# A load of down-projection weights issued as three transfers by partition range, in a decode block of attention and gated MLP

## The chip, the cores and the metric

The kernel runs on one core of one Trainium2 chip. The metric is the device time of one execution in microseconds; before the change it is 1279.16, the median of 3 runs (1279.07 to 1279.24). The engines are named as in the profile: PE does matmuls (PEld is its weight load), DVE and ACT are the vector and scalar engines, POOL is GpSimd, and SP only issues DMAs and waits. Data moves between HBM and SBUF (128 partitions) over 16 DMA engines.

## The reference

One token for each of 4 batch rows goes through attention over a cache of 8192 keys, with 32 heads of 128, and then through a gated MLP of width 1792. Both parts add to their input.

```python
def _A_ref(x, k_cache, v_cache, wq, wo):
    B, Sq, D = x.shape                      # 4, 1, 512
    H, Dh = 32, 128
    q = (x @ wq).reshape(B, Sq, H, Dh).transpose(0, 2, 1, 3)
    scores = jnp.einsum("bhqd,bhkd->bhqk", q, k_cache) * (Dh ** -0.5)
    p = _softmax(scores, axis=-1)
    o = jnp.einsum("bhqk,bhkd->bhqd", p, v_cache)
    return o.transpose(0, 2, 1, 3).reshape(B, Sq, H * Dh) @ wo

def _B_ref(x, w_gate, w_up, w_down):
    g = jnp.einsum("bsd,df->bsf", x, w_gate)
    u = jnp.einsum("bsd,df->bsf", x, w_up)
    return jnp.einsum("bsf,fd->bsd", _sigmoid(g) * u, w_down)

h = x + _A_ref(_layernorm(x), ...)
h2 = h + _B_ref(_layernorm(h), ...)
```

All inputs are bf16. The two caches are 268 MB each and make up nearly all of the bytes.

## The kernel before

The 128 pairs of batch row and head are worked off in 32 units of 4 heads. For each unit the keys (8 MB) and the values (8 MB) are loaded by one DMA each (L538) into one of three slots of the buffer KV; each partition gets 64 KB in one run. DVE transposes the keys in 16 steps (L334), PE makes the scores (L343), ACT the exponentials (L368), and PE multiplies with the values (L404) one unit later. All loads are issued by SP, in the order of one list, each as soon as its slot is free; a load waits in the DMA queue behind the bytes that were issued before it.

At the end the slots are used again for weights. When the last unit's keys have been read, SP issues the output projection (L543), the gate weights (L545) and the up weights (L549) into slot 1. When the values of the unit before the last have been read, it issues the down weights into slot 2 (L554). In SBUF the down weights are 14 tiles of 128 partitions by 512 columns, `wd_v`; partition p holds rows 14p to 14p + 13 of the matrix, 1 KB each. The tuple `WDT = (0, 8, 12, 14)` cuts them into three loads: tiles 0 to 7, 8 to 11 and 12 to 13, or 8 KB, 4 KB and 2 KB for each partition. Each has a semaphore of its own, `t_wd[i]`, and a DMA that has landed adds 16 to its semaphore. The last values are in slot 0 and are read after that.

After the attention the rest is a chain of small steps: output projection (L474), sum and layer norm (L479 to L286), gate (L493) with its sigmoid on ACT (L504), up projection, product and transposes in two halves on DVE (L510, L513), and the down projection on PE, line L518: 28 matmuls, two for each of the 14 tiles, one for each half of the 512 output columns, placed side by side in the array. A tile's matmuls wait for the half of the transposed product that they need and for the load that brings the tile:

```python
for t in range(NFT):
    if t == 0:
        filler(4)
    t_d = emit("pe", down(t), [t_hh[2 * t // NFT], t_wd[[t < v for v in WDT[1:]].index(True)]], incs=2)
```

So tiles 0 to 7 wait for the first load, 8 to 11 for the second, 12 and 13 for the third. DVE then adds the residual (L526), and two small DMAs, one issued by SP and one by ACT (L556), write the output. `prog.token(key, by)` makes a pair of a semaphore and the value to wait for, `by` above the last one; `prog.dma(engine, key, fn, waits, tok)` puts a DMA on an engine's list with a completion that adds 16, and returns the token.

## Time and profile before

| | before |
|---|---|
| median of 3 runs | 1279.16 us (1279.07 to 1279.24) |
| the profiled execution, its own time | 1279.28 us |
| span from the first to the last instruction in it | 1278.0 us |
| granted TensorE clock, mean | 0.814 |
| down weights: issue to landing of the three loads | 32.0, 32.9, 33.1 us |

The page of the profile gives busy time of each engine as a sum and by 40 slices of the span, then the DMA queues, the chain of waits that ended last, groups of instructions by line, and the DMA issues with the time from issue to landing. A busy share is a mean over stages; the chain and the windows of the last stage tell what sets the end.

### The profile page before, as it was taken

How to read it: one execution, taken by the hardware profiler on the slowest of the kernel's cores; microseconds unless marked ns; L12 is line 12 of the kernel's file. 1: busy time of each engine (PE TensorE's matmuls, PEld its weight loads, DVE VectorE, ACT ScalarE, POOL GpSimd, SP SyncE). 2: the span in 40 equal slices, each digit the busy share in tenths (PEclk: the TensorE clock that was granted, in tenths of full speed). 3: DMA queues.
4: the chain of work that ended last, by engine and by line, in shares of the span. 5: the costliest groups of instructions: out<-in, count | busy, mean ns of one | idle time of the engine just before them, and what ended most of it. 6: DMA issues, size and time to landing. Idle time of an engine off the chain costs nothing.

```text
span 1278.0 us, 14081 instructions
## 1 busy us (share of the span) xinstructions
PE 782.9 (61%) x4590; PEld 328.4 (26%) x4641; DVE 762.3 (60%) x917; ACT 58.7 (5%) x114; POOL 5.7 (0%) x22
## 2 busy tenths in 40 slices
PE   1676765557755557655567655567555576555577
PEld 0232222223222223222222222222222232222233
DVE  1876665556665557665567655566655566655571
ACT  2000000000000000000000000000000000000001
POOL 1000000000000000000000000000000000000000
PEclk8788877788877788777788777888777888777889
DMA  9999999999999999999999999999999999999998
GB/s 425 429 425 429 427 449 435 427 429 429 453 429 427 429 435 447 429 429 427 445 437 429 429 427 449 433 429 429 427 449 435 427 429 431 449 431 427 429 437 360
DMA packets 10252, 550.83 MB, mean 431 GB/s; under 512 B 1148, under 2 KB 1160, under 8 KB 1416
## 3 DMA queue, kind: packets, MB, share of 16 engines
q1 hardware_dynamic: 10232, 550.77, 99.7%
q8 instruction: 2, 0.03, 0.0%
q14 instruction: 2, 0.02, 0.0%
q10 hardware_dynamic: 16, 0.01, 0.0%
HBM read 550.77 MB, written 0.00 MB: 431 GB/s over the span
## 4 chain that ended last, share of the span: by engine, by line
DMA 60%; PE 20%; DVE 12%; issue 2%; ACT 1%; SPq 0%; DVEq 0%
DMA KV<-in_A_k_cache_dram 58%; PE PS L343 15%; DVE kT L334 12%; PE PS L404 5%; DMA KV<-in_B_w_down_dram 3%; ACT kT L409 1%; PE PS L414 0%; SPq L538 0%; DVE PTz L374 0%; PE PS L518 0%; DVE KV L526 0%; SPq L554 0%; DVEq L112 0%
## 5 line engine op out<-in xcount | busy, mean ns | idle before, releaser
L343 PE MATMUL PS<-kT,Lq 128*128 128x512 bf16 x2048 | 592.0, 422 | 342.6 <-DVE kT L334 325.5
L334 DVE STREAM_TRANSPOSE kT<-KV 128x1024 f32<-128x1024 f32 x512 | 614.2, 1231 | 302.7 <-DMA KV<-in_A_k_cache_dram 237.9
L343 PEld LDWEIGHTS PS<-kT,Lq 128*128 x2048 | 211.0, 103 | 696.4 <-issue 624.2
L374 DVE STREAM_TRANSPOSE PTz<-E_sb 32x512 bf16<-32x512 bf16 x128 | 89.9, 703 | 128.9 <-PE PS L414 125.2
L404 PE MATMUL PS<-KV,PTz 128*16 128x512 bf16 x2048 | 116.9, 381 | 0.0
L378 PE MATMUL PS<-part,headw 128*128 128x2 f32 x64 | 18.8, 363 | 100.5 <-DVE PTz L374 100.5
L368 ACT ACTIVATE E_sb<-PS,negm 128x512 bf16<-128x512 f32 x32 | 22.0, 687 | 1141.7 <-DVE negm L366 1141.7
L404 PEld LDWEIGHTS PS<-KV,PTz 128*16 128x16 bf16 x2048 | 57.7, 109 | 57.3 <-issue 13.6
L414 PE MATMUL PS<-lane,kT 128*128 128x4 f32 x256 | 33.6, 255 | 31.0 <-ACT kT L409 31.0
L361 DVE TENSOR_REDUCE part<-PS 128x1 f32<-128x512 f32 x32 | 22.1, 691 | 38.8 <-PE PS L343 38.8
L414 PEld LDWEIGHTS PS<-lane,kT 128*128 128x128 f32 x256 | 31.0, 191 | 46.3 <-issue 44.9
L378 PEld LDWEIGHTS PS<-part,headw 128*128 128x128 f32 x64 | 16.0, 311 | 103.7 <-DVE PTz L374 103.7
L409 ACT ACTIVATE kT<-PS,rsb 128x512 f32<-128x512 f32 x32 | 22.0, 687 | 64.3 <-PE PS L404 64.3
L387 PE MATMUL PS<-Lq 128*128 128x512 bf16 x33 | 12.1, 425 | 2.7 <-issue 2.0
L453 DVE TENSOR_TENSOR kT<-PS,mask 128x512 bf16<-128x512 f32 x1 | 0.7, 690 | 16.1 <-PE PS L414 16.1
L327 DVE TENSOR_TENSOR Lq<-q_all,mask 128x32 bf16<-128x32 bf16 x32 | 9.7, 302 | 0.0
L387 PEld LDWEIGHTS PS<-Lq 128*128 128x128 bf16 x53 | 5.5, 109 | 8.9 <-issue 5.1
L366 DVE STREAM_TRANSPOSE negm<-mxr 128x32 f32<-128x32 f32 x32 | 6.8, 212 | 1.1
L363 DVE STREAM_TRANSPOSE turn<-part 128x32 f32<-128x32 f32 x32 | 6.8, 212 | 1.1
L395 DVE RECIPROCAL rsb<-PS 128x1 f32<-128x1 f32 x32 | 6.5, 202 | 0.7 <-PE PS L378 0.7
L321 PEld LDWEIGHTS PS<-Lq,headw 128*128 128x128 bf16 x32 | 3.4, 106 | 12.7 <-issue 11.2
L364 DVE TENSOR_SCALAR_CACHE_REDUCE turn<-turn 128x32 f32<-128x32 f32 x32 | 6.0, 186 | 1.1
(67 smaller groups left out, 52.6 us busy)
## 6 DMA issues: line engine op xcount, KB each, us to landing
KV<-in_A_wq_dram SPq DMA_DIRECT2D x1, 4096.0 KB, 12.4
KV<-in_A_wo_dram SPq DMA_DIRECT2D x1, 4096.0 KB, 26.9
KV<-in_B_w_gate_dram SPq DMA_DIRECT2D x1, 1792.0 KB, 31.0
KV<-in_B_w_up_dram SPq DMA_DIRECT2D x1, 1792.0 KB, 34.8
KV<-in_B_w_down_dram SPq DMA_DIRECT2D x1, 1024.0 KB, 32.0
KV<-in_A_k_cache_dram SPq DMA_DIRECT2D x32, 49.7
KV<-in_A_v_cache_dram SPq DMA_DIRECT2D x32, 30.8
KV<-in_B_w_down_dram SPq DMA_DIRECT2D x1, 512.0 KB, 32.9
```

Of the source, the lines that this page charges most:

```text
L327: t_lq[u] = emit("dve", lambda e, ix: e.tensor_tensor(dst, bass.AP(raw(q_all), at(ix, 0) * (4 * TU) + 4 * (u - TU * t), [[NU * 4, 128], [1 ...
L334: t_tr[u, c] = emit("dve", lambda e: e.transpose(kT[:, (c % 2) * TW:(c % 2 + 1) * TW], KVw[:, o:o + TW]), w, ch="d2p")
L343: ins = e.matmul(bank[SBK], bass.AP(raw(Lq), ix[-1] * 2 + (128 * t + c % 2), [[528, 128], [1, 128]]), rhs, start=False, stop=False, skip_g ...
L361: a = emit("dve", lambda e: e.tensor_reduce(part[:, 0:1], bank[SBK], AX.X, ALU.max), [t_sc[u, NT - 1], t_pool], ch="d2d")
L363: a = emit("dve", lambda e: e.transpose(turn_[:, :], part[:, :]), [a], ch="d2d")
L368: t_exp[u] = emit("act", lambda e: e.activation(E_sb[:, :], bank[SBK], ACT.Exp, bias=negm[:, 0:1], scale=SCALE, accum_out=part[:, 1:2]), [ ...
L374: return [e.transpose(PTz[32 * q:32 * (q + 1), :].rearrange("p (r q c) -> p r q c", r=4, q=4)[:, :, q, :], E_sb[32 * q:32 * (q + 1), :].re ...
L378: t_sum[u] = emit("pe", lambda e: e.matmul(bank[QB[1]][:, 0:2], headw[:, :], part[:, 0:2], start=True, stop=True), [t_ptz[u], t_selc], ch= ...
L387: emit("pe", lambda e: [e.matmul(bank[XS], Lq[:, 0:128], Lq[:, 0:512], start=True, stop=True) for _ in range(n)][-1], [t_ps0, t_lq[NU - 1] ...
L404: made.append(e.matmul(PS[32 * j:32 * j + 16, ob:ob + 512], lhsT, KV[:, slot * SLOT + 512 * k:slot * SLOT + 512 * (k + 1)], start=(k < 4), ...
L409: t_ocp[u] = emit("act", lambda e: e.activation(O_sb, bank[OBK], ACT.Copy, scale=rsb[:, 0:1]), [t_pv[u], t_rs[u]], ch="a2p")
L414: ins = e.matmul(bass.AP(raw(PS), at(ix, 0) * 4 + (512 * EX + 4 * (u - t)), [[4096, 128], [1, 4]]), O_sb[:, 128 * q:128 * (q + 1)], lane[: ...
```

## The change

The second load of the down weights, tiles 8 to 11, is issued as three DMAs in a row, of partitions 0 to 63, 64 to 115 and 116 to 127. All three add to the semaphore of the second load, whose token is now for 16 x 3 = 48. The first and the third load are one DMA each as before. The bytes, their places in SBUF, the waits ahead of the issues and the order of the instructions on the other engines are the same; SP has two instructions more.

```diff
-        t_wd = [prog.token(f"wd{i}", 16) for i in range(len(WDT) - 1)]
+        WDP = [(0, 128), (0, 64, 116, 128), (0, 128)]
+        t_wd = [prog.token(f"wd{i}", 16 * (len(WDP[i]) - 1)) for i in range(len(WDT) - 1)]
...
         for i in range(len(WDT) - 1):
-            prog.dma("sp", f"wd{i}", lambda e, i=i: e.dma_start(
-                wd_v[:, WDT[i]:WDT[i + 1], :], wd_src[:, WDT[i]:WDT[i + 1], :]), [v_done], tok=t_wd[i])
+            for a, b in zip(WDP[i], WDP[i][1:]):
+                prog.dma("sp", f"wd{i}", lambda e, i=i, a=a, b=b: e.dma_start(
+                    wd_v[a:b, WDT[i]:WDT[i + 1], :], wd_src[a:b, WDT[i]:WDT[i + 1], :]), [v_done], tok=t_wd[i])
```

## The prediction

> **What bounds the kernel now.** I read four views in this order: the profile's page for the whole span, the chain of waits over the last 37 us, the DMA issues, and short windows of the end for what the DMA engines still do there. The page first: the busy shares, the row by slices, the queues and the total.

> ```profile
> span 1278.0 us, 14081 instructions
> PE 782.9 (61%) x4590; PEld 328.4 (26%) x4641; DVE 762.3 (60%) x917; ACT 58.7 (5%) x114; POOL 5.7 (0%) x22
> DMA  9999999999999999999999999999999999999998
> q1 hardware_dynamic: 10232, 550.77, 99.7%
> q10 hardware_dynamic: 16, 0.01, 0.0%
> HBM read 550.77 MB, written 0.00 MB: 431 GB/s over the span
> ```

> The DMA engines are at 9 tenths or more in 39 of 40 slices and in the fortieth at 8; no compute engine is above 61%. The kernel is as long as its bytes, and then as the few us between the last byte and the last instruction. The change leaves every byte as it is, so only those few us are open. The chain of waits shows them (start us, length us, what):

> ```profile
> 1240.44 0.70 ACT kT L409
> ...
> 1241.70 0.33 SPq L554
> 1242.02 0.04 issue
> 1242.07 32.92 DMA KV<-in_B_w_down_dram
> 1274.98 0.04 issue
> 1275.03 0.60 PE PS L518 x8
> 1275.63 0.04 issue
> 1275.67 0.43 PE PS L518 x4
> 1276.10 0.02 issue
> 1276.12 0.42 DVE KV L526
> ```

> The second load of the down weights is itself a link: issued at 1242.07, it lands at 1242.07 + 32.92 = 1274.99, and 8 matmuls that wait for it (tiles 8 to 11) start at 1275.03. The last 4 (tiles 12 and 13) start at 1275.67. The DMA issues tell whether they waited for their own load (out<-in, queue, count, KB, us to landing), and the instructions in order of time give the issues' own places:

> ```profile
> KV<-in_B_w_down_dram SPq DMA_DIRECT2D x1, 1024.0 KB, 32.0
> KV<-in_B_w_down_dram SPq DMA_DIRECT2D x1, 512.0 KB, 32.9
> KV<-in_B_w_down_dram SPq DMA_DIRECT2D x1, 256.0 KB, 33.1
> ```

> ```profile
> 1241.70 1.28 SPq L554 DMA_DIRECT2D KV<-in_B_w_down_dram  x3
> 1273.87 2.18 PE L518 MATMUL PS<-KV 128*4 128x256 bf16 x28 [0.68 <-DMA KV<-in_B_w_down_dram]
> 1275.03 0.31 PEld L518 LDWEIGHTS PS<-KV 128*4 128x4 bf16 x8 [0.41 <-DMA KV<-in_B_w_down_dram]
> 1275.67 0.09 PEld L518 LDWEIGHTS PS<-KV 128*4 128x4 bf16 x4 [0.33 <-DMA KV<-in_B_w_down_dram]
> 1276.56 0.35 SPq L556 DMA_DIRECT2D out_dram<-KV  x1
> ```

> The first load lands at 1241.70 + 32.0 = 1273.7 and the third, issued some 0.85 us into the 1.28 us of the three issues, at 1242.55 + 33.1 = 1275.65: both later groups of matmuls wait for DMA, for 0.41 and 0.33 us by the idle time of the weight loads. What sets the end is therefore the last DMA engine to finish the second load and then the third. How many engines is that? Windows of the tail give the mean share of the 16 engines in use (the number ahead of GB/s; the DMA share times 16 is the number of engines):

> ```profile
> 1273.40:1273.80 0.40, 0.00 (x0) 0.00 (x0) 0.36 (x2) 0.00 (x0) 0.00 (x0) 1.00 0.74 282
> 1273.80:1274.20 0.40, 0.33 (x7) 0.30 (x9) 0.17 (x1) 0.00 (x0) 0.00 (x0) 1.00 0.32 123
> 1274.20:1274.50 0.30, 0.30 (x10) 0.26 (x6) 0.00 (x0) 0.00 (x0) 0.00 (x0) 1.00 0.16 61
> 1274.50:1274.90 0.40, 0.40 (x8) 0.10 (x3) 0.00 (x0) 0.00 (x0) 0.00 (x0) 1.00 0.13 51
> 1275.10:1275.30 0.20, 0.20 (x6) 0.16 (x8) 0.00 (x0) 0.00 (x0) 0.00 (x0) 1.00 0.03 10
> ```

> 0.74 is 12 engines, 0.32 is 5, 0.16 is 2.6 and 0.13 is 2.1. So some twelve engines are through with everything near 1274.0, and two run on alone to about 1275.2. The end waits for two late engines; the others have about 1.1 us to spare. This is the picture on which everything below rests.

> **The change, part by part.** Two more issues on SP. One of the three issues costs 1.28 / 3 = 0.43 us, so two add 0.86 us to SP, which then ends its issues near 1243.8. The transfers land 30 us later behind queued bytes, and SP's next instruction, the output's issue, is at 1276.56: cost nothing. The cover is the load's wait in the queue of 32 us; without it the third load would start 0.86 us late. Nothing is queued behind a new wait: SP gets none, and PE waits at the same place for one semaphore, at 48 in place of 16.

> The rows per engine. Transfers of 128 partitions are even: the page's 10232 packets on queue 1 are 71 loads of 128 rows and 16 completions (71 x 144 = 10224) and 8 packets of the output. The load of x, 4 partitions, used 4 engines:

> ```profile
> DMA packets 24, 0.53 MB, mean 264 GB/s; under 512 B 4, under 2 KB 8, under 8 KB 8
> q10 hardware_dynamic: 8, 0.00, 0.7%
> ```

> These are the first 3 us: 8 packets on the queue of that load, 4 rows and 4 completions. I take it that a load is dealt in equal shares to as many engines, up to 16, as divide its rows: 64 rows go as 4 to each of 16, 52 as 4 to each of 13, 12 as 1 to each of 12. [...] Against 8 rows each before, twelve engines get 9, one gets 8, three get 4. A row of the second load is 4 tiles of 512 bf16, 4096 B; an engine moves 431 / 16 = 26.9 GB/s, so a row takes 0.152 us. Twelve engines are 0.15 us longer, three are 4 x 0.152 = 0.61 us shorter.

> Which engines are the two late ones? No view numbers them. By count alone both are among the three relieved with 3/16 x 2/15 = 1/40, and at least one is among the twelve lengthened in 1 - 4/16 x 3/15 = 19 of 20. So the value that I take is: a late engine gets one row more. Landing of the second and of the third load +0.15 us, both groups of matmuls with it, and what follows (0.43 + 0.02 + 0.42, then the output) as it is. The 25 completions more, at most two an engine, have no price in any row; not counted.

> The pace of a piece that covers part of the partitions is not in the trace. Below: no loss, an engine's 26.9 GB/s holds, the sum above. Above: a piece goes at the full 431 GB/s times its share of the 128 partitions; then each of the three takes as long as the whole did, 524288 B / 431 GB/s = 1.22 us, 3.65 us in place of 1.22, that is +2.4 us for an engine in the middle of it. I take a value near the lower end, +0.2 instead of +0.15, since the late engines pass when the body has left. Body engines start the load together and could hinder one another, but have 1.1 us to spare; a late engine comes 1.1 us behind them.

> [...]

> Sum: +0.2 us on the profiled execution's own 1279.28 (its span of 1278.0 and 1.28 around it). That execution stands 0.12 above the median of the runs, 1279.16; on the median the forecast is 1279.35.

> **The rivals.** First, *both late engines are the relieved ones*. They finish the second load 0.61 us sooner. But PE then sets the pace: 8 matmuls, four pairs side by side, take 0.60 us with 0.27 of it the last one's duration (272 ns):

> ```profile
> L518 PE MATMUL PS<-KV 128*4 128x256 bf16 x28 | 2.0, 272 | 0.8 <-DMA KV<-in_B_w_down_dram 0.7
> ```

> a pair each (0.60 - 0.27) / 3 = 0.11 us. Fourteen pairs from 1273.87 without a wait end at 1273.87 + 13 x 0.11 + 0.27 = 1275.57; now they end at 1276.10. So at most 0.5 us is to be had: 1278.65. For it: two engines alone make the tail. Against it: three engines of sixteen must be the right ones.

> Second, on the other side, *the pieces run at a part of the rate*: the body engines crowd into the same part of SBUF, first the 16 together, then 13, then 12. Price: up to +2.4 us on the body, which is done near 1274.0 to 1274.1, so 1276.4 to 1276.5 in place of 1275.2: +1.3 us, 1280.45. It decides from 1.1 us of hindrance; with the 1.7 us that lies halfway between 1.1 and the upper end the time is +0.6, 1279.8. If the late engines are hindered as much as the body, the whole +2.4 us counts: 1281.55. For it: the loads now use all partitions at once and run at 431 GB/s, so nothing shows a spare rate. Against it: the engines are spread over 1.1 us, and pieces of different parts overlap.

> Third, *the pieces go to few engines*: 52 rows on 4 engines are 13 each; with 4 and 3 of the other pieces 20 in place of 8, 12 x 0.152 = 1.8 us; the body comes to 1275.9, +0.7, and if a late engine is one of them +1.8: 1279.85 to 1280.95. On one engine, 52 + 12 + 4 = 68 rows, 60 x 0.152 = 9.1 us: about +8, 1287. Against it: the load of x, split evenly.

> Fourth, *nothing to be seen*: the late engines keep their 8 rows, or the 0.15 falls in the scatter of 1279.07 to 1279.24: 1279.16.

> **How the numbers follow.** A late engine gets a row more, with little hindrance (the forecast, 1279.35): 0.45, and nothing to be seen 0.10. Both relieved: 0.12. Part of the rate: 0.25, of which 0.04 at the far end. Few engines: 0.08, of which 0.03 at one engine. The range goes from the first rival's 1278.65 to 1280.3, where the second's middle and the mild end of the third lie within; above it are about 0.10, below it a few hundredths. A difference under 0.2% (2.56 us) is about what a measurement of this kernel can tell from no change. No case is faster by as much, since PE alone stops the gain at 0.5 us: 0.02 for what I don't see. Slower by as much are one engine, and the far end of the second with something added: 0.03 + 0.04 = 0.07. Within it the rest, 0.91.

> **What would show it.** The packets of queue 1 tell the dealing: 64 + 16 + 52 + 13 + 12 + 12 = 169 in place of 144, so 10257 in all; 10240 would be 4 engines. The window of 1274.5 to 1274.9 tells the late engines: about 2 engines as now, with the tail some 0.15 us longer, if they got a row more; under 1 if both were relieved; 6 or more if the body was held up. The chain should still end through the second and third of the loads and PE, with 8 matmuls at about 1275.2. The forecast is wrong if the weight loads of tiles 8 to 11 no longer wait for DMA, or if the share between 1273.4 and 1274.2 is far above 0.74 and 0.32.

## The result and the profile after

The changed kernel takes 1281.39 us, median of 21 runs (1280.88 to 1282.2); the kernel before, run beside it, 1279.31 (1279.07 to 1279.94). The ratio is 1.0016, 95% interval 1.0011 to 1.0022: slower by 2.1 us, and no run of the one falls among the runs of the other. The forecast was +0.2 us with a range to 1280.3. The profiled execution of the changed kernel took 1281.94 us, 0.55 above its median.

The page of the changed kernel, in two of the rows shown of before:

```profile
span 1280.7 us, 14083 instructions
q1 hardware_dynamic: 10257, 550.77, 99.6%
```

Two instructions more, the same bytes, 25 packets more. The chain of waits at its end (start us, length us, what):

```profile
1241.70 33.84 DMA KV<-in_B_w_down_dram
1275.54 0.14 issue
1275.68 3.19 PE PS L519 x28
1278.87 0.02 issue
1278.89 0.42 DVE KV L527
```

Two things are new. The load at the head of the chain is now the first one (issued at 1241.70), which the change does not touch. It lands at 1275.54; before, it landed at 1273.73. And all 28 matmuls now stand in one piece of 3.19 us, which was 8 in 0.60 and 4 in 0.43 at the end of a group that began at 1273.87. The windows of the end show what the DMA engines do meanwhile (us, then busy time and count of PE, PEld, DVE, ACT, POOL, the granted clock, the DMA share, GB/s):

```profile
1272.00:1273.00 1.00, 0.84 (x7) 0.31 (x4) 0.62 (x2) 0.01 (x1) 0.00 (x0) 1.00 1.17 180
1273.40:1273.80 0.40, 0.00 (x0) 0.00 (x0) 0.36 (x2) 0.00 (x0) 0.00 (x0) 1.00 0.78 200
1273.80:1274.20 0.40, 0.00 (x0) 0.00 (x0) 0.10 (x1) 0.00 (x0) 0.00 (x0) 1.00 1.05 220
1274.50:1274.90 0.40, 0.00 (x0) 0.00 (x0) 0.00 (x0) 0.00 (x0) 0.00 (x0) 1.00 0.87 143
```

In 1272 to 1273 the kernel before moved 424 GB/s:

```profile
1272.00:1273.00 1.00, 0.84 (x11) 0.31 (x4) 0.55 (x2) 0.13 (x1) 0.00 (x0) 1.00 1.05 424
```

Now the DMA engines are as busy (share 1.17) and move 180. From 1274.5 to 1274.9, where two engines were left, 0.87 x 16 = 14 are at work. So the engines do not wait; each packet takes longer, as the counts below show. Both signs that the prediction named for being wrong are there: the share between 1273.4 and 1274.2 is 0.78 and 1.05 for 0.74 and 0.32, and the matmuls of tiles 8 to 11 no longer stand apart. Windows of a full us from the same view tell of PE:

```profile
1274.00:1275.00 1.00, 0.00 (x0) 0.00 (x0) 0.00 (x0) 0.00 (x0) 0.00 (x0) 1.00 0.85 156
1275.00:1276.00 1.00, 0.32 (x4) 0.25 (x6) 0.00 (x0) 0.00 (x0) 0.00 (x0) 0.64 0.46 131
1276.00:1277.00 1.00, 1.00 (x14) 0.62 (x10) 0.00 (x0) 0.00 (x0) 0.00 (x0) 0.50 0.16 61
```

PE had nothing to do from 1273.1 to 1275.68. The clock that it was granted fell to 0.50 during this wait, near 1275.3 (0.64 is the mean of the window from 1275 to 1276), and was still there when its matmuls ran. The group shows the price, and the length of the wait:

```profile
L519 PE MATMUL PS<-KV 128*4 128x256 bf16 x28 | 3.1, 414 | 2.6 <-DMA KV<-in_B_w_down_dram 2.6
```

A matmul takes 414 ns where it took 272.

Where the packets' time went can be counted in the trace by size: 8192 B rows (one packet each) belong to the first load, 4096 B to the second, 2048 B to the third. Nanoseconds of one packet, median / 90th percentile / longest, and the us at which the sixteen engines completed the first load:

```
                8192 B          4096 B          2048 B
before          313/319/321     159/169/172      84/ 89/ 94
after           314/332/853     294/426/486     144/200/248

first load, completions 1 to 12, and the last four
before          1272.07 to 1272.55     1272.85  1272.94  1273.57  1273.73
after           1271.84 to 1272.62     1274.01  1274.17  1275.25  1275.54
```

Twelve engines finish the first load as before. The four late ones are still in it while the twelve are in the pieces. Nine rows of the first load began after 1272.0, and all nine ended after 1272.62, so they belong to the late engines: they took 493 to 853 ns, where the last nine before took 309 to 321. The last row ended at 1274.71 for 1273.31, and its completion came 0.83 us behind it for 0.42: together that is the hold-up of 1.8 us.

### The profile page after: what moved, and what is told of

Its sections match the earlier page's. It is cut to its first block, busy times and chain, and to the rows that moved or that the text cites. A ratio compares the mean times of both kernels' runs of the same rounds, so it can differ in the third digit from the quotient of the medians.

```text
span 1280.7 us, 14083 instructions
## 1 busy us (share of the span) xinstructions
PE 780.8 (61%) x4590; PEld 328.7 (26%) x4641; DVE 763.2 (60%) x917; ACT 58.7 (5%) x114; POOL 5.7 (0%) x22
## 3 DMA queue, kind: packets, MB, share of 16 engines
q1 hardware_dynamic: 10257, 550.77, 99.6%
HBM read 550.77 MB, written 0.00 MB: 430 GB/s over the span
## 6 DMA issues: line engine op xcount, KB each, us to landing
KV<-in_A_wo_dram SPq DMA_DIRECT2D x1, 4096.0 KB, 26.9
KV<-in_B_w_down_dram SPq DMA_DIRECT2D x1, 1024.0 KB, 33.8
KV<-in_B_w_down_dram SPq DMA_DIRECT2D x2, 256.0 KB, 34.0
```

## The experiments

Each was run beside the kernel before; the time of that is 1279.23 in all. The 95% intervals of the ratios are about 0.001 to each side (1.2 us), so for differences under that the verdict rests on landings and packets of the profiled execution and on whether the ranges of the runs overlap. The kernel before took 1278.98 to 1280.46 in all of these; the runs with partitions 0 to 63, the third load, the 12 rows and 32 to 95 first overlap that range.

**Three transfers over all partitions.** The number of issues and the shared semaphore of the change, without its cut by partitions.

```diff
-WDP = [(0, 128), (0, 64, 116, 128), (0, 128)]
+WDP = [(0, 8), (8, 10, 11, 12), (12, 14)]
...
-wd_v[a:b, WDT[i]:WDT[i + 1], :], wd_src[a:b, WDT[i]:WDT[i + 1], :]
+wd_v[:, a:b, :], wd_src[:, a:b, :]
```

> The second load as three transfers on one semaphore again, but each over all 128 partitions (tiles 8 and 9, tile 10, tile 11). Theory (a piece that covers part of the partitions crowds the engines, which also slows the late engines that still work on the first load): here nothing is crowded, the first load lands near 1273.8 us as before the change, the time is that of before within 0.3 us. Rival (three issues and three completions on one semaphore cost by themselves): about +2 us, as in the changed kernel.

Measured: 1279.21 (1279.12 to 1279.42), ratio 0.9999 (0.999 to 1.0009). The first load landed at 1273.68 and the chain ends as before:

```profile
1242.35 32.62 DMA KV<-in_B_w_down_dram
1274.98 0.04 issue
1275.02 0.60 PE PS L519 x8
```

So two more issues and a wait for 48 cost nothing that shows; the cut by partitions costs it all.

**Halves.** No engine gets more rows than another: from 1235 us on there are 136 packets under 512 B for 120 before, the 16 completions of one more load on 16 engines.

```diff
-WDP = [(0, 128), (0, 64, 116, 128), (0, 128)]
+WDP = [(0, 128), (0, 64, 128), (0, 128)]
```

> Two pieces, partitions 0 to 63 and 64 to 127; every engine has 4 + 4 rows as before, none is lengthened or relieved. Theory (crowding): the first load still lands 1.5 us or more late, at 1275.2 or after, and PE starts its down matmuls after 2.3 us or more of idle; +1.2 to +2.2 us. Rival (the loss comes from the twelve engines with a ninth row): no difference, within 0.3 us.

Measured: 1281.41 (1280.79 to 1282.26), ratio 1.0015 (1.0005 to 1.0025), and the first load landed at 1276.39. All of the loss is there with 4 + 4 rows on every engine: the ninth row of twelve engines, and the relief of three, on which the forecast was built, can't be seen beside it.

**Partitions 0 to 63 alone, and 32 to 95 alone.** Same bytes, same rows for each engine, one transfer each; what differs is the place in SBUF, and with it which rows of the matrix are read. Both leave out half of the second load.

```diff
-WDP = [(0, 128), (0, 64, 116, 128), (0, 128)]
+WDP = [(0, 128), (0, 64), (0, 128)]         # the first
+WDP = [(0, 128), (32, 96), (0, 128)]        # the second
```

> Only partitions 0 to 63 of the second load are moved, by one transfer of 64 rows; partitions 64 to 127 of tiles 8 to 11 are left out. Half the bytes, so 0.6 us less for each engine if nothing crowds. Theory (crowding): single rows of 4096 B take up to about 0.4 us in place of 0.16, and the first load lands 0.8 us or more later than before. Rival (64 rows as such are no slower): the first load lands near 1273.75, the second and third 0.6 us sooner, and the time is 0.3 to 0.5 us under before.

> As the kernel with partitions 0 to 63 alone, but the 64 rows are partitions 32 to 95; the others of tiles 8 to 11 are left out. [...] Rival (any piece of 64 rows crowds, by its number of partitions): the same as with partitions 0 to 63, the first load 0.8 us or more late.

Measured: 1279.99 (1279.5 to 1280.23) and 1278.79 (1278.53 to 1278.95); the ranges lie 0.55 us apart. With 0 to 63 the 4096 B rows took 241 ns in the median and 461 at most, and the first load landed at 1274.65; with 32 to 95 they took 159 and 169, and it landed at 1273.76. In the chains of both kernels, the first and then the second, no load but the first is left:

```profile
1241.42 33.23 DMA KV<-in_B_w_down_dram
1274.65 0.14 issue
1274.78 1.74 PE PS L519 x28
```

```profile
1241.88 31.88 DMA KV<-in_B_w_down_dram
1273.76 0.14 issue
1273.89 1.74 PE PS L519 x28
```

So of two pieces of 64 partitions one was slow, with 241 ns a row, and one was not, with 159 ns: it is not the number of partitions in a piece that counts, but which they are. Whether SBUF or the reading from HBM makes the difference, no run separates; the halves of the up weights below, which are another matrix, were slow as well (172 to 229 GB/s).

**The changed kernel with PE kept busy.** 16 instead of 4 filling matmuls stand ahead of the down projection.

```diff
         if t == 0:
-            filler(4)
+            filler(16)
```

> The changed kernel with 16 instead of 4 idle-time matmuls ahead of the down projection (about 3.4 us of them, to near 1275.6), so that PE is not idle while it waits for the first load. Theory: in the changed kernel PE's granted clock fell to 0.50 because it had been idle for 2.6 us, and the 28 matmuls at that clock, 3.2 us, set the end. With the filling the clock stays at 1.00, the matmuls wait for the third load near 1277.6 and end 0.43 us after it: 0.6 to 0.9 us under the changed kernel, 1280.5 to 1280.8. Rival (the end is set by the landings alone, the clock is a side effect): no difference from the changed kernel, 1281.4.

Measured: 1281.06 (1280.78 to 1281.6), ratio 1.0013 (1.0004 to 1.0022). The clock stayed at 1.00, and the end went back to waiting for the loads:

```profile
1243.15 34.26 DMA KV<-in_B_w_down_dram
1277.41 0.04 issue
1277.46 0.60 PE PS L519 x8
```

The mechanism was as expected; the median is 0.33 us under the changed kernel's, about half of what was expected, and the ranges overlap. It was run again with the changed kernel next to it on one chip:

> The changed kernel once more, beside its copy with 16 filling matmuls, on one chip. Theory (idle PE costs it the full clock): +2.0 to +2.3 us over before, and 0.3 us or more above the copy with the filling. Rival (the clock is a side effect): the same time as the copy, within 0.15 us.

> The copy with 16 filling matmuls ahead of the down projection, on the same chip. Theory: clock at 1.00 to the end, +1.6 to +1.9 us over before. Rival: +2.0 to +2.3 us, as without.

Measured: 1281.79 (1280.86 to 1282.39) without, 1281.39 (1281.06 to 1282.51) with the filling, ratios 1.0019 and 1.0018 with overlapping intervals. The medians differ by 0.40, but the ranges overlap, and both expectations of the time were missed: +2.6 for +2.0 to +2.3 without, +2.2 for +1.6 to +1.9 with. The clock did what was said: 0.50 from 1276 to 1278 in the one, 1.00 to the end in the other:

```profile
1276.00:1277.00 1.00, 1.00 (x14) 0.59 (x12) 0.00 (x0) 0.00 (x0) 0.00 (x0) 0.50 0.24 88
```

```profile
1276.00:1277.00 1.00, 0.97 (x16) 0.65 (x16) 0.00 (x0) 0.00 (x0) 0.00 (x0) 1.00 0.21 51
```

The late landings alone cost 1.8 us or more, since with a full clock the kernel is still that much slower. What the half clock adds, these runs do not settle. The medians say 0.3 to 0.4 us. In the profiled execution of the changed kernel the third load landed at 1277.62 and the matmuls ended at 1278.87; with the last four in 0.43 us, as before, they would have ended near 1278.1, so the estimate from its chain is 0.8. But in the two filled executions the third load landed at 1278.04 and 1278.20, 0.4 to 0.5 later than in their partners; why is open.

**The same cut on the third load.** Half as many bytes, and further from the first load.

```diff
-WDP = [(0, 128), (0, 64, 116, 128), (0, 128)]
+WDP = [(0, 128), (0, 128), (0, 64, 116, 128)]
```

> The second load is one transfer again, the third (tiles 12 and 13, half as many bytes) comes as the same three pieces. [...] Rival (each split costs about the same wherever it is): +2 us.

Measured: 1279.75 (1279.59 to 1280.18), +0.5 us. The first load landed 0.5 us late, at 1274.25, the second at 1275.84. That is a quarter of the loss for half the bytes. It fits that the late engines were nearer to the end of the first load by then, but this is argued.

**Only the 12 rows of partitions 116 to 127.** 116 rows of the second load are left out.

```diff
-WDP = [(0, 128), (0, 64, 116, 128), (0, 128)]
+WDP = [(0, 128), (116, 128), (0, 128)]
```

> Of the second load only the piece of partitions 116 to 127 is moved, 12 rows; partitions 0 to 115 of tiles 8 to 11 are left out. [...] Rival of the prediction (a piece has the full rate times its share of the 128 partitions): 12 rows take 1.2 us, as long as the whole load did. [...]

Measured: 1279.34 (1278.98 to 1279.82). The rival missed the rows: the twelve took 159 to 185 ns each, where it had 1200. The crowding showed beside them: 2048 B rows took 91 ns in the median and up to 214 where they took 84, and 8192 B rows up to 621. Nine of the twelve began within 0.4 us and the other three 1.2 us or more later, so there was perhaps too little at one time to slow them; that is argued and not shown. Nor did the 116 rows left out bring a gain (1279.34 for 1279.23): the first load landed at 1274.06, 0.3 late, and in this execution the compute before the down projection was later still, as its chain shows:

```profile
1273.75 0.42 DVE KV L514
1274.20 1.74 PE PS L519 x28
```

**Partitions 32 to 95 first, then 0 to 31 and 96 to 127.** The whole load in three pieces, of which the first, moved alone, was not slow (159 ns a row).

```diff
-WDP = [(0, 128), (0, 64, 116, 128), (0, 128)]
+WDP = [[(0, 128)], [(32, 96), (0, 32), (96, 128)], [(0, 128)]]
...
-for a, b in zip(WDP[i], WDP[i][1:]):
+for a, b in WDP[i]:
```

> Three pieces that move the whole second load: partitions 32 to 95 first, then 0 to 31, then 96 to 127; 4, 2 and 2 rows for each engine. [...] Rival (three pieces of partitions cost as they do in the changed kernel): +2 us.

Measured: 1279.99 (1279.76 to 1280.57), +0.76, with a median of 172 ns for a row and 319 at the 90th percentile; the first load landed at 1274.41. In order of their starts the first 58 rows took 159 to 176 ns, about as before the change, and the 70 behind them up to 368: 64 rows belong to 32 to 95, so within one load the rows turn slow about where the pieces change. A third of the loss, with half the bytes in the two pieces behind.

**The up weights in halves.** The kernel before, with its up load cut at partition 64. The down weights' loads are whole.

```diff
-t_wu = [prog.token(f"wu{i}", 16) for i in range(len(WUC) - 1)]
+t_wu = [prog.token(f"wu{i}", 32) for i in range(len(WUC) - 1)]
...
-reg(1, 16384 + (NC + WUC[i]) * F, ...), wu_src[:, WUC[i] * F:WUC[i + 1] * F]
+for a, b in ((0, 64), (64, 128)):
+    reg(1, 16384 + (NC + WUC[i]) * F, ...)[a:b, :], wu_src[a:b, WUC[i] * F:WUC[i + 1] * F]
```

> The kernel before, with the up weights' load (1792 KB, 3.5 times the second load of the down weights) as two transfers of partitions 0 to 63 and 64 to 127; the down weights' loads are whole. [...] Rival (the loss is the one-time hold-up of the late engines at the end and does not grow with the bytes): +2.2 us or less.

Measured: 1287.29 (1286.7 to 1288.65), ratio 1.0064 (1.0049 to 1.0079): +8.1 us, where the rival had at most 2.2. For twelve us, from 1265 to 1277, the queue ran at 172 to 229 GB/s, about half of the 431 over the span of before, with busy engines:

```profile
1265.00:1267.00 2.00, 1.23 (x13) 0.24 (x6) 0.00 (x0) 0.60 (x1) 0.00 (x0) 0.61 1.09 172
1275.00:1277.00 2.00, 0.00 (x0) 0.00 (x0) 0.00 (x0) 0.00 (x0) 0.00 (x0) 0.50 0.96 210
```

Half the rate for the up load alone would be 4.26 us more (an estimate: 1792 KB at 431 GB/s). But its halves slow the loads in front and behind as well: 8192 B rows of the first down load took 576 ns in the median for 313, and the gate load landed at 1269.60 where it landed near 1266.95. The third down load landed at 1282.2 for 1275.62, 6.6 us late; PE, idle for 6.4 us, then ran at a clock of 0.50, with 2.66 us for its 28 matmuls.

## Why the prediction was wrong

The dealing of rows was right: queue 1 has 10257 packets, 25 more than before, as many as the completions of 13 and of 12 engines for the two further pieces; the semaphore of the second load got 41, which is 16 + 13 + 12. But that the twelve are among the thirteen, from which the sum takes twelve engines with a ninth row and three relieved, no run shows: the runs show how many engines a piece has, not which, and the halves lost as much with 4 + 4 rows on every engine. The free issues and the wait for 48 were right, by the three transfers over all partitions. That two late engines end the tail was right in kind: four late engines, 0.3 to 1.2 us behind the twelfth, can be counted in the completions.

The step that failed is the price of a piece that covers part of the partitions: "I take a value near the lower end, +0.2 instead of +0.15, since the late engines pass when the body has left." The pieces of the twelve engines that are on time (the prediction's body) did not meet the late engines in the second load but in the first. While the twelve put the second load into a part of the partitions, the late ones were still writing the first load, and their rows took 493 to 853 ns there. The first load landed 1.8 us late, a term that the sum had at nothing: the prediction had the first load end the same and looked only at the loads behind it. The lag was taken for a cover; it was the exposure. That a crowded piece slows the rows beside it is shown by the three transfers over all partitions and by the runs with 0 to 63 and 32 to 95, where the first load landed at 1273.68, 1274.65 and 1273.76; at what place the engines meet is argued, since no run here numbers an engine, and the pieces differ in the rows read as well.

The second rival had the mechanism, at a chance of 0.25. Its price of up to 2.4 us on the body was of the right size: the twelfth engine completed the third load at 1276.30 for 1274.47, 1.8 us late. Its time of 1280.45 was too low because it too let the late engines pass. Its far end, "If the late engines are hindered as much as the body", 1281.55, is within 0.2 us of the measured 1281.39; it had 0.04. That it comes so near is in part luck, since it has the late engines held up in the second load and no slower clock.

The granted clock was not among the terms. It fell to 0.50 while PE waited 2.6 us for the first load, and the 28 matmuls took 3.19 us for 1.74 (the run with partitions 32 to 95). This hides part of what the second and third load's landings would cost, since PE is then busy while they land. The length of the wait alone does not decide it. With the halves PE was idle for 2.9 us, and the clock fell at 1277.7, 1.2 us after its matmuls had begun; with partitions 0 to 63 alone it was idle for 1.85 us, and the clock stayed. What the traces show beside it: in those of the kernel before and the changed one the granted clock keeps each value for 1 to 8 times 3.41 us (but for the last stretch, which the end cuts off), and at the end of these kernels it fell after a stretch of 3.41 us in which PE had been busy for 1.09 us (the changed kernel), 1.27 (the same again), 1.14 (the halves) or 1.42 (the up weights in halves), and stayed after one with 1.56 (0 to 63 alone). The busy time alone does not decide it either: in the changed kernel the clock also fell at 1203.59, after a stretch of 3.41 us with 1.85 us of busy PE. What does, the runs do not show.

The first rival's bound held: without any wait for the later loads PE's 28 matmuls take 1.74 us, and the kernel with partitions 32 to 95 alone was 0.44 us under before; the prediction had said at most 0.5. Whether any of the three relieved engines is a late one stays open, since no run here numbers the engines; the halves, which relieve none, took the same time. What makes four engines late was not tried. No version was found that moves all bytes and beats the kernel before.

## What to carry to other kernels

In this queue, which moved 431 GB/s over its span, a load cut by partitions was not neutral (1281.39 for 1279.31), and with the same rows on every engine it lost as much (1281.41 for 1279.23): ask which partitions all engines write at the same moment, and price the cut on the loads in front of it and behind it too. Cut by columns, over all partitions, three transfers cost nothing that shows (1279.21 for 1279.23). A lagging engine wasn't safe from what the others did next (493 to 853 ns a row for 309 to 321), and a wait of 2.6 us ahead of the last matmuls went with a clock of 0.50 besides.
